# Moving one weight-conversion step behind two output copies in a hand-written engine schedule

## The chip, the cores and the metric

The kernel runs on one core of a Trainium2 chip. The metric is the device time of one execution in microseconds (us). Three executions of the kernel before took 1083.78, 1084.74 and 1087.2 us; the median is 1084.74 us.

## The reference

Eight batches of 576 tokens by 512 channels go through three stages:

```python
# attention without a score matrix, 8 heads of 64
q_s = softmax(q, over the head dimension);  k_s = softmax(k, over the tokens)
x = q_s @ (k_s.T @ v)
# first mixer
h = relu(x @ w_in); u, v = h[..., :512], h[..., 512:]
v_n = (v - mean(v)) / sqrt(var(v) + 1e-6)
y1 = (u * (w_spatial @ v_n + b_spatial)) @ w_out
# second mixer
theta = y1 @ w_theta
u = y1 + w_tok_r @ (y1 * cos(theta)) + w_tok_i @ (y1 * sin(theta))
out = u + relu(u @ w_ch)
```

Several weight matrices (`w_in`, `w_out`, `w_theta`, `w_tok`, `w_ch`) are doubles and are sent as their bits; the kernel turns each block of such a matrix into two float32 halves, `hi` and `lo`.

## The kernel before

Each float32 product is made of three passes over such halves (hi by hi, hi by lo, lo by hi). Two phases follow each other. The first runs over the eight batches; in batch b it does the first mixer of batch b and the attention of batch b + 1, with parts of the attention of batch b + 2, and it sends `y1` to DRAM. The second phase runs the second mixer over all batches from there. This study is about the first phase.

The order of all work is written out by hand: each batch has a string of words, and one word stands for one step, a Python function that issues instructions to several engines. Every engine takes its own instructions in the order in which the words issue them. Batch 0 runs `PLANS[0]`, batch 1 `PLANS[1]`, batches 2 to 6 `PLAN` and batch 7 `LAST`. The steps that matter here:

- `Y0` to `Y3` (`y_mm`, helper line 164): the products with `w_out`, 24 matrix products (of 288 columns) each, into a PSUM tile of two banks. The pool of these tiles has three buffers, shared by all large products (`V`, `K`, `U`, `S`, `T`, `X`, `Y`).
- `y0` to `y3` (`y_out`, L555 and L556): ScalarE copies the PSUM tile of `Yi` to SBUF, into one of nine buffers of a pool called `t2`, and SyncE's queue sends it to DRAM. The copy is what frees the PSUM tile.
- `X3` and `x3` (L164; L437, L438, L456): a product of the attention, and its split by a ScalarE copy and VectorE operations. `X1`, `x1`, `X2` and `x2p` are alike; with the flag `p`, ScalarE also copies the tile out of PSUM (L435) and GpSimd does the subtraction.
- `B` (`Convert.bits`, lines 214 to 245): the first step of a weight block's conversion. In the form used here VectorE does L219, L225, L229 and L241, and ScalarE L223 (behind L219) and L232 (behind L229); L241 comes behind L223. It takes three `t2` buffers. Then `bits` lets SyncE's queue load the block that will be wanted two steps later (L212).
- `P0v` and `P` (`Convert.parts`): the second step of a conversion: ScalarE L257, VectorE L258 and the product L261, which VectorE does with the flag `v` and GpSimd without; for blocks kept for the second phase two DMAs to DRAM follow (L263, L264).
- `ksub2` (L321, L326) and `qsub2` (L399): large subtractions on GpSimd; `kmb2` (L313) a ScalarE copy ahead of `ksub2`; `qmax2` (L394) a VectorE reduction ahead of `qsub2`; `kexp2` (L333) and, in the next batch, `qexp1` (L402) exponentials on ScalarE behind them.
- `V0`, `V1`, `V2`, `K1` open the next batch on TensorE (L172 and L350); `v0` to `v2` (L477) are the ScalarE copies that free their tiles.

In `PLAN` the batch ends with "... `G3v P0v kbc2 kmb2 ksub2 Y0 B Y1 y0 X3 x3 y1 qmax2 qsub2 Y2 kexp2 Y3 y2 P0v y3`". There are 35 weight blocks in all, and each `B` takes the next one; by the count of the words they are used up within batch 6, before the `B` between `Y0` and `Y1`, which then does nothing. Batch 6 also has no `kmax2` to `kexp2`, since there is no batch 8.

Of the kernel before, what the change touches and what calls it, by code (L numbers as in the profile page):

```python
# [17 lines left out]
P = 128  # L18
MAGIC = 12582912.0
# [4 lines left out]
HALF_PI = 1.5707963267948966  # L24
# 896 float32 exponents: a double's bias less a float32's.
REBASE = -896.0 * 2**23


# The first phase's schedule.
KCUTS = (0, 2048, 1024, 1536)  # L30
# [11 lines left out]
)  # L42
# [23 lines left out]
def kernel(  # L66
# [12 lines left out]
):  # L79
    """float32 products run as three float32r passes: x = hi + lo with hi = x rounded to  # L80
    float32r and lo = x - hi (exact), and x @ y = hi@hi + hi@lo + lo@hi."""
    nc = tc.nc
    B = q.shape[0]
    S = w_tok.shape[2]
# [14 lines left out]
    def psum(two, one):  # L99
        """PSUM for a phase: `two` buffers of two banks, `one` of a single bank."""  # L100
        pools.close()
        for n, bufs in (("two", two), ("one", one)):
            ps_now[n] = pools.enter_context(
                tc.tile_pool(name=f"ps_{n}{two}", bufs=bufs, space=bass.MemoryType.PSUM)
            )
# [9 lines left out]

    # Buffers of the first phase; the second one takes them over when they fall free.
    w4_all = fix.tile([P, 8, 1024], F32R, name="w4")
# [41 lines left out]
    def acc(ps, pairs, first=True, final=True):  # L159
        """ps += lhsT.T @ rhs over the pairs, the free size in two halves."""  # L160
        last = len(pairs) - 1
        for i, (a, w) in enumerate(pairs):
            for c in range(2):
                nc.tensor.matmul(  # L164
                    out=ps[:, c, 0:CH], lhsT=a, rhs=w[:, c * CH:(c + 1) * CH],
                    start=first and i == 0, stop=final and i == last,
                )
# [11 lines left out]

# [1 line left out]
    class Split:  # L181
        """A float32 matrix from DRAM, split: hi and lo are where the halves go."""

# [15 lines left out]
    class Convert:  # L199
        """A double matrix from DRAM, given as its bits, split. The exponent, rebased as a number  # L200
        (below float32's range it comes to zero), and the first 11 mantissa bits are hi; the other
        bits, times hi's power of two, are lo."""

# [61 lines left out]

# [1 line left out]
    def load(to, x, n, cuts=(0,)):  # L267
        """The columns from each cut to the next."""
        if n < B:
            ends = sorted(cuts)[1:] + [x.shape[2]]  # L270
            for c in cuts:
                e = ends[sorted(cuts).index(c)]
                nc.sync.dma_start(out=to[:, c:e], in_=x[n][:, c:e])
# [42 lines left out]
    def k_sub(n, hs, eng):  # L316
        """Half h: heads 4h to 4h + 3."""
        mb = st["mb"]
        c = slice(hs[0] * 256, (hs[-1] + 1) * 256)
        km = kb[:, 0:2048].rearrange("p (r c) -> p r c", r=NT)[:, :, c]  # L320
        eng.tensor_tensor(  # L321
            out=km, in0=km, in1=mb[:, :, c].to_broadcast([P, NT, c.stop - c.start]), op=ALU.subtract
        )
        for h in hs:
            p0, c0 = h * 64, h * 256
            eng.tensor_tensor(  # L326
                out=kb[p0:p0 + 64, 2048:2304], in0=kb[p0:p0 + 64, 2048:2304],
                in1=mb[p0:p0 + 64, 0, c0:c0 + 256], op=ALU.subtract,
            )
# [100 lines left out]
    def split(ps, h, l, eng):  # L430
        """ps as hi and lo; GpSimd, which has no way to PSUM, needs a copy."""
        if eng is nc.gpsimd:
            x = t2()
            x = halves(x) if len(ps.shape) == 3 else x
            nc.scalar.copy(out=x, in_=ps)  # L435
            ps = x
        nc.scalar.copy(out=h, in_=ps)  # L437
        eng.tensor_tensor(out=l, in0=ps, in1=f(h), op=ALU.subtract)  # L438

    def q_t_split(n, j, eng):  # L440
        ps = st.pop(("T", j))
        # The first batch has a buffer more, where w_out comes later.
        h, l = qt_s[j % 2 * 2:j % 2 * 2 + 2] if n or j < 2 else [w[:, 0:S] for w in wo[j * 2 - 4:j * 2 - 2]]
        split(ps[:, 0:S], h, l, eng)
        st["qt", j] = h, l
# [11 lines left out]

# [1 line left out]
    def v_mm(t):  # L459
# [97 lines left out]

# [1 line left out]
    y1 = [t.rearrange("p (k s) -> p k s", k=NK) for t in (qb, kb)]  # L559
    z_rem = [vn[8:10]]  # L560

    def zs(b, t):
        """(hi, lo) of zr and of zi. The first batch's come while the first phase still needs
        w_out, some of them where w_ch comes after them."""
        if t < 2:
            z = vn[4 * t:4 * t + 4]
        else:
            z = [w[:, 0:DM] for w in w4[4 * t - 8:4 * t - 4]]
            if b:
                z = [w[:, h * DM:(h + 1) * DM] for w in wo[2 * t - 4:2 * t - 2] for h in range(2)]  # L570
        return z[0:2], z[2:4]
# [15 lines left out]

    # The last tokens of two batches share a tile.
    def load_rem(b):
# [28 lines left out]
    def th_whole(b, t):  # L618
        """Whole turns in theta, plus MAGIC."""
        ps = th[b, t]  # L620
        r, w = t2(DM), t2(DM)
        nc.scalar.activation(out=w, in_=ps, func=ACTF.Copy, scale=INV_2PI, bias=MAGIC)
        th[b, t] = ps, r, w

    def th_turns(b, t):
        """theta less whole turns, in [-pi, pi]."""
        ps, r, w = th[b, t]
        nc.vector.tensor_scalar(out=w, in0=w, scalar1=-MAGIC, scalar2=None, op0=ALU.add)
        nc.vector.scalar_tensor_tensor(out=r, in0=w, scalar=-TWO_PI_HI, in1=ps, op0=ALU.mult, op1=ALU.add)
        nc.vector.scalar_tensor_tensor(out=r, in0=w, scalar=-TWO_PI_LO, in1=r, op0=ALU.mult, op1=ALU.add)  # L630
        nc.vector.tensor_scalar(
            out=r, in0=r, scalar1=PI_BELOW, scalar2=-PI_BELOW, op0=ALU.min, op1=ALU.max
        )
        th[b, t] = r, w
# [49 lines left out]
    def theta(b, i):  # L684
        """Step i of a batch's theta: the products of tile i, and what follows them for the tiles
        before it."""
        if b < B:
            for lag, part in (
                (3, th_y), (0, th_mm), (1, th_whole), (2, th_trig), (4, th_hi),
                (3, th_z), (1, th_turns), (4, th_lo),  # L690
            ):
                if 0 <= i - lag < NT + (b % 2 == 0):
                    part(b, i - lag)

    def tok_mm(b, m, part=None):
        """In parts: the products whose weights come first, the others."""
        c = slice(m * P, (m + 1) * P)
# [23 lines left out]
    def ch_mm(b, m):  # L721
# [5 lines left out]
        if (b, m) != (B - 1, NK - 1):  # L727
# [6 lines left out]
            return  # L734
        # The very last: half of it is on its way while the other half is computed.
        for c in (slice(0, CH), slice(CH, S)):
# [8 lines left out]
    w_out_k = w_out.rearrange("k p f -> p k f")  # L745
    # The first phase's weights; ORDER has them in the order in which it needs them.
    w1 = {}
# [10 lines left out]
    first = [w1[n] for n in ORDER.split()]  # L758
    # The second phase's, kept in DRAM until their buffers fall free.
    later = [  # L760
# [18 lines left out]

    # A batch's schedule is made of words NAME[DIGIT[FLAGS]]. DIGIT is a tile, or for the  # L780
    # attention's own steps the batch's distance. Flags: v and p have a step done by the vector
    # engine or by GpSimd, a and b one half of it.
    def eng(fl, other=nc.gpsimd):
# [102 lines left out]
def _rows(a):  # L886
    """[B, H, S, D] -> [B, 128, R]: whole tiles of 128 tokens as (tile, head, d), then the
    last 64 tokens, heads 0-3 on partitions 0-63 and heads 4-7 on partitions 64-127."""
    import numpy as np
# [8 lines left out]
def _rows_v(a):  # L898
    """The same tokens with a one after each head's row; the last tile holds each head's rows
    on the partitions where q and k have them and zeros on the others."""  # L900
    import numpy as np
# [59 lines left out]
```

## Time and profile before

| | |
|---|---|
| timed executions | 1083.78, 1084.74, 1087.2 us |
| profiled execution, span from the first to the last instruction | 1082.7 us |
| median of the timed executions less that span | 2.0 us |
| TensorE busy / weight loads | 94% / 88% of the span |
| VectorE / ScalarE / GpSimd busy | 62% / 39% / 35% |
| mean granted TensorE clock | 0.972 |

The profiled execution is known by its span; its own time with what lies around the span is not given, and the timed executions are 1.1 to 4.5 us above the span. The granted clock is a share of full speed, 2.4 GHz; the other level is 1.2 GHz. Busy shares are averages over stages with different limits, so the stage at a batch's end is read by itself.

### The profile page before, as it was taken

To read this page: it belongs to the slowest core of one execution; us is meant where nothing else is said; L and a number is where in the kernel's file an instruction comes from. 1 tells how busy PE (TensorE), PEld (TensorE's weight loads), DVE (VectorE), ACT (ScalarE), POOL (GpSimd) and SP (SyncE) were. 2 spreads that over 40 slices of the span, in tenths; PEclk is the share of its full clock that TensorE was granted. 3 is DMA by queue.
4 is the path that set the end of the run, shared out by engine and by line. 5 is a ranking of instruction groups with operands and counts; after the bars stand their busy time and mean duration, and the time that the engine had idled before them with its cause. 6 is when DMAs were issued, how large, how long until landed. Compare 5 with 4: busy or idle time off the path is not lost.

```text
span 1082.7 us, 16227 instructions
## 1 busy us (share of the span) xinstructions
PE 1018.7 (94%) x6688; PEld 952.1 (88%) x6688; DVE 674.9 (62%) x971; ACT 420.1 (39%) x674; POOL 383.7 (35%) x287
## 2 busy tenths in 40 slices
PE   4777799999898998998999999999999999999998
PEld 3666789989798898898999989999999899989998
DVE  7988847866767668677642582738473746366532
ACT  3644345444443353344432461415141424152310
POOL 5466515542444334434521241413131213222220
PEclk9878899999999899998999999999999999999999
DMA  8442122422342233413015041702020101011011
GB/s 278 142 136 99 61 88 121 169 115 86 110 159 77 91 146 107 157 58 131 3 49 185 24 166 76 175 1 74 15 77 22 56 34 65 33 49 41 1 45 44
DMA packets 37369, 96.49 MB, mean 89 GB/s; under 512 B 7088, under 2 KB 15792, under 8 KB 33200
## 3 DMA queue, kind: packets, MB, share of 16 engines
q1 hardware_dynamic: 33744, 85.96, 22.0%
q0 software_dynamic: 3552, 9.50, 3.1%
q8 instruction: 52, 0.85, 0.3%
q14 instruction: 21, 0.17, 0.0%
HBM read 67.08 MB, written 28.38 MB: 88 GB/s over the span
## 4 chain that ended last, share of the span: by engine, by line
PE 72%; DVE 5%; issue 3%; ACT 1%; ACTq 0%
PE ps L164 50%; PE pb L172 10%; PE ps L172 7%; PE ps L350 3%; PE pb L646 1%; DVE t L282 1%; PE ps L425 1%; DVE t L258 1%; DVE t L287 1%; DVE t L219 0%; DVE t L225 0%; PE ps L427 0%; DVE t L539 0%; ACT t L555 0%; DVE t L229 0%
## 5 line engine op out<-in xcount | busy, mean ns | idle before, releaser
L164 PE MATMUL ps<-sp,vn 128*128 128x288 f32 x1472 | 212.6, 301 | 7.0 <-ACT vn L505 3.0
L164 PEld LDWEIGHTS ps<-sp,vn 128*128 128x128 f32 x1472 | 203.5, 193 | 9.1 <-ACT vn L505 3.4
L164 PE MATMUL ps<-g,wo 128*128 128x288 f32 x1104 | 169.7, 308 | 19.8 <-ACT t L555 19.7
L164 PEld LDWEIGHTS ps<-g,wo 128*128 128x128 f32 x1104 | 159.9, 200 | 21.7 <-ACT t L555 21.1
L719 POOL TENSOR_TENSOR qt<-u,uh 128x576 fp32r<-128x576 f32 x31 | 44.2, 1427 | 218.0 <-ACT uh L717 218.0
L717 ACT CAST uh<-u 128x576 fp32r<-128x576 f32 x32 | 21.6, 674 | 216.3 <-DVE u L714 216.3
L172 PE MATMUL ps<-w,xh 128*128 128x512 f32 x320 | 100.6, 408 | 2.9 <-ACT w L257 2.9
L164 PE MATMUL ps<-xh,w 128*128 128x288 f32 x512 | 92.7, 300 | 4.1 <-ACT w L257 2.3
L164 PE MATMUL ps<-uh,w 128*128 128x288 f32 x496 | 91.8, 299 | 0.0
L164 PEld LDWEIGHTS ps<-xh,w 128*128 128x128 f32 x512 | 77.5, 191 | 6.1 <-ACT w L257 2.9
L172 PE MATMUL pb<-w,xh 128*128 128x512 f32 x256 | 81.3, 398 | 0.0
L172 PEld LDWEIGHTS ps<-w,xh 128*128 128x128 f32 x320 | 61.0, 194 | 17.8 <-ACT w L257 3.2
L541 POOL TENSOR_TENSOR g<-t,g 128x576 fp32r<-128x576 f32 x24 | 35.9, 1494 | 112.0 <-ACT g L540 93.0
L164 PEld LDWEIGHTS ps<-uh,w 128*128 128x128 f32 x496 | 73.6, 188 | 0.3
L488 POOL TENSOR_TENSOR mv<-mv,neg_half 128x1 f32<-128x1 f32 (+1 forms) x40 | 27.1, 688 | 125.4 <-DVE mv L487 117.2
L714 DVE TENSOR_TENSOR u<-ps,kb 128x576 f32<-128x576 f32 x16 | 12.1, 758 | 74.0 <-PE ps L164 74.0
L484 DVE BATCH_NORM_STATS2 sm<-t 128x6 f32<-128x512 f32 (+1 forms) x40 | 27.3, 684 | 47.3 <-ACT t L477 41.7
L172 PEld LDWEIGHTS pb<-w,xh 128*128 128x128 f32 x256 | 47.0, 188 | 9.9
L164 PE MATMUL ps<-xl,w 128*128 128x288 f32 x256 | 55.5, 299 | 0.0
L540 ACT CAST g<-t 128x576 fp32r<-128x576 f32 x32 | 21.5, 673 | 84.8 <-DVE t L539 84.8
L164 PE MATMUL ps<-sp,wo 128*128 128x288 f32 x336 | 53.8, 296 | 0.0
L164 PE MATMUL ps<-qt,w 128*128 128x288 f32 x248 | 53.0, 295 | 0.0
(203 smaller groups left out, 2081.9 us busy)
## 6 DMA issues: line engine op xcount, KB each, us to landing
vb<-in_v SPq DMA_DIRECT2D x8, 1300.0 KB, 7.0
y<-t SPq DMA_DIRECT2D x32, 288.0 KB, 2.1
out<-t SPq DMA_DIRECT2D x31, 288.0 KB, 2.1
qb<-in_q SPq DMA_DIRECT2D x7, 1152.0 KB, 5.0
kb<-in_k SPq DMA_DIRECT2D x6, 1152.0 KB, 7.9
st<-in_w_tok SPq DMA_DIRECT2D x9, 576.0 KB, 4.1
tok_d<-st SPq DMA_DIRECT2D x18, 288.0 KB, 2.1
qb<-y SPq DMA_DIRECT2D x4, 1152.0 KB, 5.2
```

What stands on the lines that cost most here:

```text
L164: nc.tensor.matmul(out=ps[:, c, 0:CH], lhsT=a, rhs=w[:, c * CH:(c + 1) * CH], start=first and i == 0, stop=final and i == last,)
L172: nc.tensor.matmul(out=ps, lhsT=a, rhs=w, start=(i == 0), stop=(i == last))
L258: nc.vector.tensor_scalar(out=w.bitcast(I32), in0=a.bitcast(I32), scalar1=-0x800000, scalar2=None, op0=ALU.bitwise_and)
L282: nc.vector.tensor_tensor(out=m[p0:p0 + 64, c0:c0 + 256], in0=m[p0:p0 + 64, c0:c0 + 256], in1=kb[p0:p0 + 64, 2048:2304], op=ALU.max,)
L350: nc.tensor.matmul(out=o, lhsT=kb[p, c0:c0 + P], rhs=v4[p, r, 2 * j:2 * j + 2, :].rearrange("p h e -> p (h e)"), start=(r == 0), stop=(r = ...
L484: nc.vector.bn_stats(out=bs[0:n], in_=vr[0:n])
L488: nc.gpsimd.tensor_tensor(out=mv[0:n, 1:2], in0=mv[0:n, 1:2], in1=neg_half[0:n, 0:1], op=ALU.pow)
L540: nc.scalar.copy(out=g_s[m], in_=g)
L541: eng.tensor_tensor(out=g_s[4 + m], in0=g, in1=f(g_s[m]), op=ALU.subtract)
L714: nc.vector.tensor_tensor(out=halves(u_s[m]), in0=ps[:, :, 0:CH], in1=halves(y1[b % 2][:, m, :]), op=ALU.add)
L717: nc.scalar.copy(out=st["uh"][:, m, :], in_=u_s[m])
L719: eng.tensor_tensor(out=qt_s[m], in0=u_s[m], in1=f(st["uh"][:, m, :]), op=ALU.subtract)
```

## The change

In `PLAN` and in `PLANS[0]` the word `B` is taken from its place ahead of `y0` (`PLAN`) or between `y0` and `y1` (`PLANS[0]`) and put behind `y1`. `PLANS[1]` and `LAST` stay. No step is added or removed. The diff also blanks comments and docstrings, line for line, so that line numbers stay.

```diff
 PLAN = (
...
-    "t3p kr2 S3 G3v P0v kbc2 kmb2 ksub2 Y0 B Y1 y0 X3 x3 y1 qmax2 qsub2 Y2 kexp2 Y3 y2 P0v y3 "
+    "t3p kr2 S3 G3v P0v kbc2 kmb2 ksub2 Y0 Y1 y0 X3 x3 y1 B qmax2 qsub2 Y2 kexp2 Y3 y2 P0v y3 "
 )
 PLANS = {
     0: (
...
-        "x0 T1 kt2 kr2 Y0 t1p kbc2 kmb2 T2 t2 ldv2 y0 B ksub2 Y1 X1 y1 P X2 x1 x2p Y2 y2 T3 ldq2 Y3 "
+        "x0 T1 kt2 kr2 Y0 t1p kbc2 kmb2 T2 t2 ldv2 y0 ksub2 Y1 X1 y1 B P X2 x1 x2p Y2 y2 T3 ldq2 Y3 "
         "t3p X3 y3 x3 qmax2 qsub2v "
     ),
```

## Rows read from the trace of the kernel before

**Rows 1.** The page: span, busy times, and one line of its DMA issues (KB each, us to landing).

```profile
span 1082.7 us, 16227 instructions
...
PE 1018.7 (94%) x6688; PEld 952.1 (88%) x6688; DVE 674.9 (62%) x971; ACT 420.1 (39%) x674; POOL 383.7 (35%) x287
...
st<-in_w_tok SPq DMA_DIRECT2D x9, 576.0 KB, 4.1
```

**Rows 2.** Waits of PE, 60 to 600 us: total us, times, longest.

```profile
PE ps L164 <- ACT t L555: 19.5, 5, 4.1
```

**Rows 3.** Chain that ended last, end of batch 2: start, us, what.

```profile
276.00 0.97 DVE t L219
...
279.29 0.63 ACT t L555
...
288.13 8.41 PE ps L172 x36
```

**Rows 4.** Timeline of PE, ends of batches 2 to 6: start, us, instructions [idle before].

```profile
268.40 6.63 PE L164 MATMUL ps<-g,wo 128*128 128x288 f32 x48
...
279.96 8.16 PE L164 MATMUL ps<-g,wo 128*128 128x288 f32 x48 [4.14 <-ACT t L555]
...
353.29 9.13 PE L164 MATMUL ps<-g,wo 128*128 128x288 f32 x48 [4.14 <-ACT t L555]
...
427.56 7.97 PE L164 MATMUL ps<-g,wo 128*128 128x288 f32 x48 [4.14 <-ACT t L555]
...
500.38 9.00 PE L164 MATMUL ps<-g,wo 128*128 128x288 f32 x48 [3.83 <-ACT t L555]
...
561.71 6.56 PE L164 MATMUL ps<-g,wo 128*128 128x288 f32 x48
```

**Rows 5.** Timeline of ACT, end of batch 2.

```profile
277.01 0.78 ACT L223 ACTIVATE t<-t,rebase 128x576 int32<-128x576 int32 x1 [6.24 <-DVE t L219]
...
280.87 2.15 ACT L333 ACTIVATE kb<-kb 128x2304 f32<-128x2304 f32 x1
...
288.70 2.13 ACT L402 ACTIVATE qb<-qb 128x2304 f32<-128x2304 f32 x1
290.97 0.60 ACT L477 ACTIVATE t<-ps 128x512 f32<-128x512 f32 x1
```

**Rows 6.** Timeline of DVE, end of batch 2.

```profile
270.90 5.17 DVE L261 TENSOR_TENSOR st<-t,t 128x576 fp32r<-128x576 f32 x1
...
278.58 0.75 DVE L241 SCALAR_TENSOR_TENSOR t<-st,t 128x576 int32<-128x576 int32 x1
...
281.39 2.54 DVE L394 TENSOR_REDUCE q_m<-qb 128x36 f32<-128x2304 f32 x1
```

**Rows 7.** Timeline of POOL, end of batch 2.

```profile
270.85 4.62 POOL L321 TENSOR_TENSOR kb<-kb,t 128x2048 f32<-128x2048 f32 x1 [3.12 <-ACT t L313]
275.42 2.14 POOL L326 TENSOR_TENSOR kb<-kb,t 64x256 f32<-64x256 f32 x2
284.17 4.06 POOL L399 TENSOR_TENSOR qb<-qb,q_m 128x2304 f32<-128x2304 f32 x1 [6.61 <-DVE q_m L394]
```

**Rows 8.** Stretches: us, busy PE, PEld, DVE, ACT, POOL, granted clock, DMA share, GB/s.

```profile
194.84:204.00 9.16, 9.16 (x70) 9.16 (x71) 6.39 (x10) 4.04 (x8) 5.74 (x4) 1.00 0.66 237
279.96:288.12 8.16, 8.15 (x49) 8.16 (x50) 7.56 (x5) 4.27 (x5) 3.96 (x1) 0.79 0.38 145
```

**Rows 9.** Timeline of PE, end of batch 0 and, last row, end of batch 1.

```profile
127.69 3.45 PE L164 MATMUL ps<-g,wo 128*128 128x288 f32 x24
...
136.02 4.97 PE L164 MATMUL ps<-g,wo 128*128 128x288 f32 x24 [3.29 <-ACT t L555]
...
194.84 0.66 PE L294 MATMUL pb<-ident,t 128*128 128x128 f32 x4 [1.26 <-DVE t L287]
```

**Rows 10.** Timeline of ACT, end of batch 0.

```profile
135.34 0.62 ACT L555 COPY t<-ps 128x576 f32<-128x576 f32 x1
...
136.91 0.65 ACT L435 COPY t<-ps 128x576 f32<-128x576 f32 x1
```

## The prediction

> **What bounds the kernel now.** The page comes first: TensorE is busy for 1018.7 of 1082.7 us, while VectorE, ScalarE and GpSimd stay at 62% and below [rows 1]. So time is gained only where TensorE stands still or runs slowly. The table of TensorE's waits in the first phase comes next, and one line leads it: five times, 19.5 us in all, the products of line 164 waited for a ScalarE instruction of L555, the y copy [rows 2]. The timeline of TensorE says where. In each of batches 2 to 5 the 48 products of `Y2` and `Y3` begin behind an idle stretch of 4.14, 4.14, 4.14 and 3.83 us, and the fifth wait, 3.29 us, stands ahead of `Y2` in batch 0 [rows 4, 9]. Each time the PSUM tile that `Y2` needs is not yet copied out.
>
> Why is the copy late? In batch 2 `Y0` and `Y1` run from 268.40 to 275.03 [rows 4], so `Y0`, the first half, is through at about 271.7. The chain that ended last starts the copy of `y0` only at 279.29 [rows 3]. In between, ScalarE stands idle for 6.24 us until L219 on VectorE is done, and runs L223 at 277.01 [rows 5]; L219 starts at 276.00 [rows 3], because the product L261 ahead of it takes from 270.90 to 276.07 [rows 6] while GpSimd's subtraction L321 runs from 270.85 to 275.47 [rows 7]. ScalarE works in order: `y0`'s copy, whose data lie ready, is queued behind the two ScalarE instructions of `B`, and those wait for VectorE.
>
> The idle time has a second price. After it the same 48 products take 8.16, 9.13, 7.97 and 9.00 us, against 6.56 us in batch 6, where `B` has no block left and no wait comes first [rows 4]. The stretch of 8.16 us shows a granted clock of 0.79 of full speed [rows 8]: part of it ran at the lower of the two levels, 1.2 GHz. In batch 0 `Y2` alone takes 4.97 us against 3.45 us of `Y1` [rows 9].
>
> **The change in batches 2 to 5.** Nothing is added or removed. `B`'s two ScalarE instructions now stand behind the copies of `y0`, `x3` and `y1`, its four VectorE instructions behind `x3`'s, and its load behind two DMAs on SyncE's queue; GpSimd gets nothing in this form of `B`.
> - ScalarE: `y0`'s copy needs only `Y0` and a free buffer. It runs at about 271.8 to 272.4, as soon as `Y0` is through, in what is now idle time.
> - TensorE: `X3` ends at 275.82 (279.96 less 4.14) and `Y2` can follow at once. `Y3` needs `y1`'s copy: behind `x3`'s ScalarE copy that ends at about 277.1, and `Y3` wants it at 275.82 + 6.56 / 2 = 279.1. No new wait.
> - Gain of idle time: 4.14 + 4.14 + 4.14 + 3.83 = 16.25 us. Gain of speed, once no idle time comes first: 8.16 + 9.13 + 7.97 + 9.00 less 4 times 6.56 = 8.02 us. Together 24.3 us.
>
> Is the gain kept? TensorE enters `V0` 5.7 us earlier in batch 2, at 275.82 + 6.56 = 282.4 instead of 288.13 [rows 3], but the other engines do not all move by that much. `V0` to `V2` take 8.41 us [rows 3]; `K1` then wants, at 290.8, the tile that `v0`'s copy frees. That copy stands on ScalarE behind the exponential of q, that behind GpSimd's subtraction, that behind `qmax2`, that behind `B`. `B`'s four VectorE instructions take 3.3 us now, from 276.00 [rows 3] to the end of L241 at 279.33 [rows 6]; the first two run beside the end of L326 [rows 7], and are longer than L241's 0.75 us. In the new place they begin behind `x3`'s operations, at about 277.5 (an estimate: `X3`'s end at 275.82, a ScalarE copy and two VectorE operations of 0.2 to 0.75 us), when L326 ends at 277.56. At 0.75 us each they take 3.0 us, at the most the old 3.3; I take 3.0, since GpSimd is then idle. Then `qmax2` 2.54 us [rows 6] to 283.0, GpSimd 4.06 us [rows 7] from 283.2 to 287.3 (the 0.2 us as now), the exponential 2.13 us and the copy 0.60 us [rows 5]: `v0` is copied at 290.0, 0.8 us before `K1` wants it, or 0.5 us with the old 3.3. So I book nothing here, with a bound of 1.5 us a batch, should GpSimd be later. The k exponential, 2.15 us [rows 5], is behind `B` in both orders and ends before the copy of `y2` is wanted by `V1`, at 285.2.
>
> The load of a later weight block is issued about 1 us later, behind the DMAs of `y0` and `y1`. Such a load lands after 4.1 us [rows 1], and its block is wanted by the second `B` from there, in the middle of a next batch that lasts 73 us (279.96 to 353.29 in rows 4). Cost nothing; without that cover it would be the 1 us.
>
> **Batch 0.** `y1`'s copy moves ahead of `B`. It ran at 135.34 [rows 10]; `Y1` ends at 131.14 [rows 9], so it can be done at 131.8. `Y2` then starts when `X2` is through, at 132.73 (136.02 less 3.29), takes 3.45 us and ends at 136.2. But `T3` behind it needs the tile that `x2p`'s copy L435 frees. That copy, at 136.91 now [rows 10], stays behind `B`'s ScalarE work and moves only by the `y1` copy that no longer stands ahead of it, about 0.5 us: it ends at 137.1. TensorE is at `T3` at 137.1, where it now is at 136.02 + 4.97 = 141.0, or about 0.2 us earlier by the overlap of successive instructions: gain 3.7 us, where `Y2`'s wait and speed alone would give 3.29 + 4.97 - 3.45 = 4.8. Batches 1, 6 and 7 keep their order, and batch 6's moved `B` is empty.
>
> **The sum.** 24.3 + 3.7 = 28.0 us off the profiled span of 1082.7 us. The median of the timed runs lies 2.0 us above that span; I take that as constant: 1084.74 - 28.0 = 1056.7 us.
>
> **Two rules weighed.** First, the clock. A TensorE idle stretch of 1.26 us at the end of batch 1 [rows 9] is followed by 9.16 us at clock 1.00 [rows 8]; the five long ones of [rows 4, 9] are followed by slow products. I take it that the 1 us of idle time that I leave in batch 0 costs no speed. The Trainium skill, in "TensorE: Matmul & The Clock Gate", section "A second HAM failure mode: psum-queue depth-cycling", says that short idle gaps between groups of products that cycle through PSUM make the clock go back and forth; by that, products would stay slow here even where the long wait is gone. The 1.26 us row speaks against it. Second, the neighbours of `B`. L261 takes 5.17 us [rows 6] beside GpSimd's subtraction, and L241, of the same size, 0.75 us after it. The Trainium skill's "GPSIMD Engine Reference", section "8. Key points", says that GpSimd shares its SBUF interfaces with VectorE and contends with instructions that read two SBUF inputs or run in a two-port mode; by that rule a `B` that met a GpSimd subtraction in its new place would stretch in the same way, and the last rival below is what that would do.
>
> **The rivals.**
> - *The copies get buffers that are not free.* `y0` and `y1` now take their `t2` buffers ahead of `B`, so others than before. If they are those that L261 reads, `y0`'s copy waits until 276.07 and ends at 276.75, `Y2` starts at 276.8, and each of four batches loses 1.0 us: 24.0 us gained, 1060.7 us. For it: nine buffers, and L261 is late. Against it: buffers of the earlier gate steps should be free for longer.
> - *The idle time goes but the speed stays low.* Then 16.25 us in batches 2 to 5 and 3.3 us in batch 0 are gained, 19.5 us: 1065.2 us. Against it the 1.26 us row; for it nothing but the page.
> - *The change does nothing:* `Y2` is held by something that ends when the copy did. Then 1084.7 us. Against it: ScalarE's 6.24 us of idle time, with `Y0` long through.
> - *Slower: the conversion holds up `qmax2`.* If `B`'s VectorE instructions met GpSimd's subtractions in the new place and were held for all of 4.62 + 2.14 + 4.06 = 10.8 us [rows 7], `v0`'s copy would be 10.8 us later than the 290.0 above and TensorE would wait 10.8 - 0.8 = 10.0 us at `K1` in each of four batches: 40.0 less 24.3 less 3.7 = 12.0 us slower, 1096.7 us. It decides from a delay of 0.8 + 28.0 / 4 = 7.8 us on. Against it: L326 ends at 277.56, where `B` begins, and the q subtraction cannot start before `qmax2`, behind `B`.
>
> **How the numbers follow.** Forecast 1056.7 us, chance 0.72, own range 1053.5 to 1059. Buffers 0.13, speed stays low 0.08, no effect 0.04, slower 0.03. The range goes down to 1053.5, for the 0.9 us by which timed runs lie below their median and 2 us by which modelled product ends hide idle time, and up to 1063, over the buffer rival and over a `K1` wait of up to 1.5 us in four batches; it leaves out about 0.15 to 0.2. About 0.3% (3.3 us) is what a measurement of this kernel can tell from no change: faster 0.94, same 0.03, slower 0.03.
>
> **What would show it.** Right: the line of waits for L555 falls from 19.5 us to about 1 us or vanishes; the 48 products of `Y2` and `Y3` take 6.6 us at clock 1.00 in batches 2 to 5; `y0`'s copy starts within 0.3 us of the end of `Y0`; in batch 0 a wait of about 1 us for L435 stands ahead of `T3`; ends of batches are shorter by 5 to 7 us. Wrong: a wait of `K1` or `V3` for L477, a `y0` copy that starts behind L261, or a `Y2` at a clock below 1.00. The prediction fails if a later stage of the batch (the gate, `T0`, `S0`) turns out to wait for GpSimd or VectorE, which move less than TensorE does.

## The result

The changed kernel takes 1060.15 us, the median of four executions (1059.61 to 1061.09), beside 1084.32 us of the kernel before (also four): a ratio of 0.9772, with a 95% interval of 0.9758 to 0.9787. The forecast was 1056.7 us. The measured time lies outside the range that the forecast gave its own theory, 1053.5 to 1059, and inside the wide one, up to 1063, which also covers a rival and a wait at `K1`. The profiled span falls from 1082.7 to 1057.8 us, 24.9 us less where 28.0 were forecast.

The page of the changed kernel, span and busy times, beside [rows 1]:

```profile
span 1057.8 us, 16239 instructions
...
PE 1009.8 (95%) x6688; PEld 943.1 (89%) x6688; DVE 676.4 (64%) x971; ACT 419.3 (40%) x674; POOL 383.6 (36%) x287
```

TensorE's waits from 60 to 600 us (total us, times, longest us), beside [rows 2]:

```profile
...
PE ps L425 <- POOL vn L506: 1.6, 3, 0.5
PE ps L425 <- ACT t L435: 1.3, 1, 1.3
PE ps L164 <- DVE qt L438: 1.0, 4, 0.3
PE ps L164 <- ACT u L524: 0.9, 4, 0.2
...
```

The line of 19.5 us for L555 is gone. In its place stand two lines that the kernel before did not have in the steady batches, L425 behind L506 and L164 behind L524, and the 1.3 us behind L435 that the forecast left in batch 0. The line for L438, 1.0 us, is in both kernels. The longer lines, left out here, are waits of batch 0 ahead of `Y0` in both kernels; `K1` of batch 0 starts at 96.59 us before and at 96.76 us after.

The timeline of TensorE in the changed kernel, ends of batches 2 and 3, then batch 0, beside [rows 4, 9]:

```profile
264.69 6.63 PE L164 MATMUL ps<-g,wo 128*128 128x288 f32 x48
271.15 0.69 PE L164 MATMUL ps<-qt,kvh 128*128 128x288 f32 x4
...
271.95 6.56 PE L164 MATMUL ps<-g,wo 128*128 128x288 f32 x48
...
340.48 6.56 PE L164 MATMUL ps<-g,wo 128*128 128x288 f32 x48
...
132.47 3.35 PE L164 MATMUL ps<-g,wo 128*128 128x288 f32 x24
...
137.10 0.66 PE L425 MATMUL ps<-ident,qb 128*128 128x128 f32 x4 [1.28 <-ACT t L435]
```

`Y2` follows `X3` at once, and its 48 products with `Y3` take 6.56 us, the time of an undisturbed batch. The table of stretches of the changed kernel, from the first products of `Y0` to the end of `Y3` in batches 2 and 3 (us, busy PE, PEld, DVE, ACT, POOL, granted clock, DMA share, GB/s), beside [rows 8], say at which clock:

```profile
264.93:278.50 13.57, 13.57 (x103) 13.57 (x103) 12.27 (x12) 7.39 (x10) 6.56 (x3) 1.00 0.37 130
333.46:347.04 13.58, 13.58 (x104) 13.58 (x103) 12.28 (x12) 7.40 (x10) 6.56 (x3) 1.00 0.37 132
```

The timeline of ScalarE in the changed kernel, end of batch 2, beside [rows 5]:

```profile
268.21 0.64 ACT L555 COPY t<-ps 128x576 f32<-128x576 f32 x1 [1.15 <-PE ps L164]
272.15 0.64 ACT L437 CAST xh<-ps 128x576 fp32r<-128x576 f32 x1 [3.30 <-PE ps L164]
272.68 0.64 ACT L555 COPY t<-ps 128x576 f32<-128x576 f32 x1
274.23 0.78 ACT L223 ACTIVATE t<-t,rebase 128x576 int32<-128x576 int32 x1 [0.90 <-DVE t L219]
```

and that of VectorE there, beside [rows 6]:

```profile
267.19 5.17 DVE L261 TENSOR_TENSOR st<-t,t 128x576 fp32r<-128x576 f32 x1
```

VectorE's L261 takes the same 5.17 us, from 267.19 to 272.36, but `y0`'s copy no longer waits for it: it starts at 268.21, as soon as TensorE has ended `Y0`. So the rival with buffers that are not free is out as well: had the copy needed a buffer that L261 reads, it could not have started before 272.36.

Where does the rest go? The table takes the point where the V products begin on the chain that ended last as the bound of a batch. In batch 2 the chain joins them in both kernels only at the last product of `V0`, which waits 0.48 us; `V0` itself begins there at 213.87 and 210.21, which gives the same gain.

| | before | after | gained | forecast |
|---|---|---|---|---|
| chain at `V0`, batch 2 (gain of batches 0 and 1) | 217.09 | 213.42 | 3.67 | 3.7 |
| batch 2 | 71.04 | 65.08 | 5.96 | 4.14 + 1.60 = 5.74 |
| batch 3 | 74.29 | 68.54 | 5.75 | 4.14 + 2.57 = 6.71 |
| batch 4 | 73.11 | 68.53 | 4.58 | 4.14 + 1.41 = 5.55 |
| batch 5 | 73.85 | 68.42 | 5.43 | 3.83 + 2.44 = 6.27 |
| batch 6 | 66.09 | 66.58 | -0.49 | 0 |

Batches 0 to 2 give what was forecast. Batches 3 to 6 give 0.96, 0.97, 0.84 and 0.49 us less, 3.3 us together. These are the batches that begin behind a shortened end; batch 2 begins behind batch 1, which keeps its order. The middle of batch 5 shows the place, in the timeline of TensorE of the changed kernel:

```profile
447.97 0.63 PE L425 MATMUL ps<-ident,qb 128*128 128x128 f32 x4 [0.52 <-POOL vn L506]
448.53 0.27 PE L427 MATMUL ps<-ident,qb 64*128 64x64 f32 x1
449.03 3.99 PE L164 MATMUL ps<-sp,vn 128*128 128x288 f32 x28 [0.23 <-ACT u L524]
```

`T0` waits 0.52 us and `S0` 0.23 us, where the kernel before waits at neither. Read backwards, the trace gives this chain. The PSUM tile of `T0` is the one that `r1` (L524) frees, that of `S0` the one that `r2` frees. These copies stand on ScalarE behind the copies of `N3` and `N4` (L505, L508, L509), those wait for L500 on VectorE, and VectorE is late since an operation of `kn1`, L382. The timelines of VectorE and GpSimd in the changed kernel, batch 5 (the L500 shown is the last that `r1` and `r2` stand behind):

```profile
430.43 0.88 DVE L375 TENSOR_TENSOR kn<-ps,sm 64x256 f32<-64x256 f32 x2
431.33 2.71 DVE L382 TENSOR_TENSOR kvl<-kn,kvh 64x256 fp32r<-64x256 f32 x2
...
443.98 2.10 DVE L500 TENSOR_SCALAR t<-t,mv 128x512 f32<-128x512 f32 x2
...
429.25 4.06 POOL L420 TENSOR_TENSOR qb<-qb,q_s 128x2304 f32<-128x2304 f32 x1
```

and the same instructions, without L375, in the kernel before:

```profile
451.29 1.10 DVE L382 TENSOR_TENSOR kvl<-kn,kvh 64x256 fp32r<-64x256 f32 x2
...
462.38 2.10 DVE L500 TENSOR_SCALAR t<-t,mv 128x512 f32<-128x512 f32 x2
...
447.61 4.05 POOL L420 TENSOR_TENSOR qb<-qb,q_s 128x2304 f32<-128x2304 f32 x1
```

The pair of L382 ends 0.73 us behind the end of GpSimd's q multiplication L420 in both kernels (434.04 and 433.31; 452.39 and 451.66). TensorE has moved forward by more than GpSimd: TensorE goes on from `K1` 2.1 us behind the start of L420 before (449.70 and 447.61) and 0.5 us behind it after (429.74 and 429.25). So the subtraction, which comes right behind `K1`, now meets the multiplication and waits for its end: 2.71 less 1.10, 1.6 us later, of which about 1.0 us a batch reaches TensorE. On the way the lateness is passed on whole: from the end of the pair to the end of L500 it takes 12.04 us after (446.08 less 434.04) and 12.09 us before (464.48 less 452.39).

### The profile page after: what moved, and what is told of

Same layout as the page of the kernel before. It is cut to its first block, busy times and chain, and to the rows that moved or that the text cites. A ratio compares the mean times of both kernels' runs of the same rounds, so it can differ in the third digit from the quotient of the medians.

```text
span 1057.8 us, 16239 instructions
## 1 busy us (share of the span) xinstructions
PE 1009.8 (95%) x6688; PEld 943.1 (89%) x6688; DVE 676.4 (64%) x971; ACT 419.3 (40%) x674; POOL 383.6 (36%) x287
## 3 DMA queue, kind: packets, MB, share of 16 engines
q1 hardware_dynamic: 33744, 85.96, 22.6%
## 4 chain that ended last, share of the span: by engine, by line
PE 69%; DVE 8%; ACT 3%; issue 2%; ACTq 0%
PE ps L164 48%; PE pb L172 10%; PE ps L172 6%; PE ps L350 3%; PE pb L646 1%; DVE t L500 1%; DVE kvl L382 1%; DVE t L282 1%; ACT u L524 1%; ACT vn L505 1%; DVE sm L484 1%; DVE t L287 1%; DVE t L258 0%; PE ps L425 0%; DVE qt L438 0%
## 5 line engine op out<-in xcount | busy, mean ns | idle before, releaser
L164 PE MATMUL ps<-sp,vn 128*128 128x288 f32 x1472 | 213.1, 301 | 9.7 <-ACT t L477 3.8
L164 PEld LDWEIGHTS ps<-sp,vn 128*128 128x128 f32 x1472 | 203.8, 193 | 12.2 <-ACT t L477 4.3
L164 PE MATMUL ps<-g,wo 128*128 128x288 f32 x1104 | 160.1, 296 | 0.2 <-ACT t L555 0.2
L164 PEld LDWEIGHTS ps<-g,wo 128*128 128x128 f32 x1104 | 150.9, 189 | 0.7 <-ACT t L555 0.4
L717 ACT CAST uh<-u 128x576 fp32r<-128x576 f32 x32 | 21.6, 673 | 216.3 <-DVE u L714 216.3
L164 PE MATMUL ps<-xh,w 128*128 128x288 f32 x512 | 91.6, 297 | 4.8 <-POOL w L261 2.4
L164 PE MATMUL ps<-uh,w 128*128 128x288 f32 x496 | 91.8, 299 | 0.0
L164 PEld LDWEIGHTS ps<-xh,w 128*128 128x128 f32 x512 | 76.3, 188 | 6.8 <-POOL w L261 3.1
L164 PEld LDWEIGHTS ps<-uh,w 128*128 128x128 f32 x496 | 73.6, 188 | 0.3
L164 PE MATMUL ps<-xl,w 128*128 128x288 f32 x256 | 54.9, 296 | 0.0
L164 PE MATMUL ps<-sp,wo 128*128 128x288 f32 x336 | 53.8, 296 | 0.0
L164 PE MATMUL ps<-qt,w 128*128 128x288 f32 x248 | 53.0, 295 | 0.0
L714 DVE TENSOR_TENSOR u<-ps,qb 128x576 f32<-128x576 f32 x16 | 12.1, 758 | 63.5 <-PE ps L164 63.5
```

What stands on the lines that cost most here:

```text
L164: nc.tensor.matmul(out=ps[:, c, 0:CH], lhsT=a, rhs=w[:, c * CH:(c + 1) * CH], start=first and i == 0, stop=final and i == last,)
L714: nc.vector.tensor_tensor(out=halves(u_s[m]), in0=ps[:, :, 0:CH], in1=halves(y1[b % 2][:, m, :]), op=ALU.add)
L717: nc.scalar.copy(out=st["uh"][:, m, :], in_=u_s[m])
```

## The experiments

The theory has two parts. First, the order of ScalarE's queue made the stall: a y copy waits for whatever stands ahead of it there, and the slow products follow from the stall. Second, the missing 3.3 us are VectorE's subtraction held by GpSimd's multiplication. The rivals are given with each run. The kernel before, run beside the experiments, had medians of 1084.13, 1085.63 and 1084.3 us in the three groups.

**One plan at a time.** In the first kernel only `PLAN` is changed, in the second only `PLANS[0]`.

```diff
 e1, against the changed kernel
-... y0 ksub2 Y1 X1 y1 B P X2 ...
+... y0 B ksub2 Y1 X1 y1 P X2 ...
 e2, against the changed kernel
-... ksub2 Y0 Y1 y0 X3 x3 y1 B qmax2 ...
+... ksub2 Y0 B Y1 y0 X3 x3 y1 qmax2 ...
```

> The move in the steady plan alone; batch 0's plan as before. Theory (each plan's gain is its own stall and adds): batch 0 loses its 3.7 us again, so 1060.2 + 3.7 = 1063.8 us, with the 2.2 us stall of batch 0 back and no wait on a y copy in batches 2 to 5. Rival (the two moves help each other, or batch 0's gain is eaten later): 1060.2, or more than 1065.

> The move in batch 0's plan alone; the steady plan as before. Theory: 1084.3 - 3.7 = 1080.6 us, and the stalls of 4.1 us stand in batches 2 to 5 as before. Rival (batch 0's gain is given back where batch 1 waits for something else): 1084.3.

Measured: 1064.14 us (ratio 0.9817, 0.9801 to 0.9834) and 1081.48 us (0.9975, 0.9963 to 0.9987). The gains of 20.0 and 2.65 us (interval 1.4 to 4.0) add up to 22.6 us beside 24.2 of the whole change; the interval of the first, 18.0 to 21.6 us, and that of the second leave room for the rest. TensorE's waits with only `PLAN` changed:

```profile
PE ps L164 <- ACT t L555: 3.3, 1, 3.3
```

and with only `PLANS[0]` changed:

```profile
PE ps L164 <- ACT t L555: 16.3, 4, 4.1
```

Each part takes away its own stalls and leaves the other's. The stall of batch 0 is 3.3 us, as in the kernel before, and not the 2.2 us of the expectation.

**Only the first copy ahead.** The step stands behind `y0`, but ahead of `x3` and `y1`.

```diff
-... Y0 Y1 y0 X3 x3 y1 B qmax2 ...
+... Y0 Y1 y0 B X3 x3 y1 qmax2 ...
```

> In the steady plan the step stands behind the first y copy only, ahead of the next batch's x split and the second y copy. Theory (ScalarE works in order, and what it has queued ahead of a y copy decides when the next output tile may start): the first wait is gone, and the second y copy now comes some 3 us later, at 1 us or less behind the moment at which TensorE wants its buffer: a new wait of 0.5 to 2 us ahead of the fourth output tile in each of batches 2 to 5, 1062 to 1068 us. Rival (the place of the first copy alone counts): 1060.2 and no wait on a y copy.

Measured: 1065.27 us (0.9832, 0.9814 to 0.9851), 5.1 us more than the changed kernel by the medians. The waits of TensorE in this kernel:

```profile
PE ps L164 <- ACT t L555: 6.0, 4, 1.6
```

Its timeline of TensorE at the end of batch 2:

```profile
272.65 3.36 PE L164 MATMUL ps<-g,wo 128*128 128x288 f32 x24
277.58 3.46 PE L164 MATMUL ps<-g,wo 128*128 128x288 f32 x24 [1.58 <-ACT t L555]
```

Its timeline of ScalarE there:

```profile
275.78 0.68 ACT L232 ACTIVATE t<-t 128x576 f32<-128x576 uint32 x1 [1.00 <-DVE t L229]
276.37 0.62 ACT L437 CAST xh<-ps 128x576 fp32r<-128x576 f32 x1
276.89 0.64 ACT L555 COPY t<-ps 128x576 f32<-128x576 f32 x1
```

The stretch behind the wait, in the columns of the stretches above (the granted clock is 1.00):

```profile
277.50:281.00 3.50, 3.42 (x25) 3.42 (x26) 3.43 (x5) 3.16 (x4) 0.29 (x1) 1.00 0.24 91
```

The stall has moved from `Y2` to `Y3`: `y1`'s copy now stands behind L232 and starts at 276.89, where the changed kernel has it at 272.68. So it is the place in ScalarE's queue that counts, for each copy by itself, and the rival is refuted. The waits are 6.0 us, and in return the 1.6 us at `T0` are gone in the next batches; together that would be 4.4 us, and what makes up the rest was not followed. The last row adds that after 1.58 us of standing still the clock is 1.00, and the 24 products take 3.46 us, as `Y1` of batch 0 does without a wait before it [rows 9].

**Still later.** The step stands behind GpSimd's q subtraction.

```diff
-... x3 y1 B qmax2 qsub2 Y2 kexp2 ...
+... x3 y1 qmax2 qsub2 B Y2 kexp2 ...
```

> In the steady plan the step stands still later, behind the q maximum and GpSimd's q subtraction. Theory (VectorE's operations on SBUF are held up beneath a long GpSimd operation, and ScalarE's k exponential, third y copy and q exponential are queued behind the step): the third y copy comes some 5 us later and the q exponential about 2.5 us later, new waits of 2 to 6 us at the turn of each steady batch, 1068 to 1085 us. Rival (any place behind the second y copy is as good): 1060.2, or about 2 us a batch less, since the q maximum and subtraction start earlier.

Measured: 1079.52 us (0.9962, 0.9948 to 0.9977), 19.4 us more than the changed kernel, 4.8 us for each of four batches. The timeline of GpSimd in this kernel, end of batch 2:

```profile
276.37 4.05 POOL L399 TENSOR_TENSOR qb<-qb,q_m 128x2304 f32<-128x2304 f32 x1 [2.74 <-DVE q_m L394]
```

VectorE beside it:

```profile
276.43 4.31 DVE L225 TENSOR_SCALAR t<-st 128x576 int32<-128x576 int32 x1
280.77 0.76 DVE L229 SCALAR_TENSOR_TENSOR t<-st,t 128x576 int32<-128x576 int32 x1
```

ScalarE behind these:

```profile
282.22 2.11 ACT L333 ACTIVATE kb<-kb 128x2304 f32<-128x2304 f32 x1
284.23 0.62 ACT L555 COPY t<-ps 128x576 f32<-128x576 f32 x1
```

TensorE, in the next batch's `V1`:

```profile
284.90 0.73 PE L172 MATMUL ps<-w,xh 128*128 128x512 f32 x2 [3.73 <-ACT t L555]
```

Two stretches behind that wait:

```profile
285.00:288.00 3.00, 3.00 (x9) 2.38 (x10) 0.00 (x0) 3.00 (x4) 0.00 (x0) 0.66 0.78 296
288.00:292.00 4.00, 4.00 (x16) 3.18 (x15) 2.72 (x7) 1.07 (x2) 1.10 (x2) 0.83 0.21 77
```

This is the forecast's slower rival in a milder form, brought about by the order of the words. `B`'s L225 takes 4.31 us beneath the subtraction (0.45 us in the changed kernel), the k exponential and `y2`'s copy are queued behind the step, the copy starts at 284.23 instead of 278.06, and TensorE stands still for 3.73 us in the next batch's `V1`. Here the clock falls to 0.66 and 0.83 behind the wait.

**The multiplication earlier.** In `PLAN`, `qmul1` goes ahead of the third V tile's statistics, whose small GpSimd operation stood in front of it.

```diff
-... qsum1 V2 v2 qmul1 K1 ldv2 kn1 ...
+... qsum1 V2 qmul1 v2 K1 ldv2 kn1 ...
```

> The changed kernel, and in the steady plan GpSimd's q multiplication ahead of the third V tile's statistics step instead of behind it: it starts some 1 to 1.5 us earlier. Theory (the 3.3 us that the forecast lacks come from the k normalisation's subtraction on VectorE, which waits for the end of that multiplication, 2.71 us a pair where it was 1.10): the pair goes back to about 1.1 to 1.6 us, TensorE's waits of 0.5, 0.2 and 0.3 us a batch go, and the time falls by 2 to 3.3 us to 1057 to 1058. Rival (the waits come with the earlier start of the batch and have another cause): 1060.2.

> The kernel of e5 itself, beside e8 on one chip: 1056.5 to 1057 by every theory; with e5's own four runs it says what the earlier q multiplication is worth.

Measured: 1056.47 us (0.9743, 0.9726 to 0.976) and, beside the last experiment, 1057.09 us (0.9748, 0.9734 to 0.9761). The changed kernel itself was run beside the first:

> The changed kernel itself, beside e5 to e7 on one chip: 1060.2 by every theory.

It took 1060.24 us (0.9773, 0.9759 to 0.9787). Beside it the earlier multiplication is worth 3.8 us by the medians; by the ratios to the kernel before it is 3.3 us in this group and 2.7 us with the repeat. That is about the 3.3 us that were missing. VectorE and GpSimd in batch 5 of this kernel:

```profile
429.54 1.30 DVE L382 TENSOR_TENSOR kvl<-kn,kvh 64x256 fp32r<-64x256 f32 x2
...
426.05 4.05 POOL L420 TENSOR_TENSOR qb<-qb,q_s 128x2304 f32<-128x2304 f32 x1 [2.61 <-DVE q_s L415]
```

The pair is back at 1.30 us and once more ends 0.74 us behind L420 (430.84 and 430.10); the waits of `T0` are gone, and that for L524 falls from four to one, of 0.2 us. From `K1` of batch 2 to `K1` of batch 6 this kernel takes 489.45 - 219.26 = 270.19 us, the changed kernel 492.23 - 219.36 = 272.87: 2.68 us less, where the table lacks 0.96 + 0.97 + 0.84 = 2.77 us in these batches. In batch 5 all of it lies where the chain says: from the start of `K1` to the start of `S0` it is 446.23 - 422.02 = 24.21 us here and 449.03 - 423.82 = 25.21 us in the changed kernel.

**The control.** The same edit in the kernel before.

> Control: the kernel before with the same earlier q multiplication as in e5. Theory (there the multiplication ended just as the k subtraction began, so nothing is held up): 1084.3, the same. Rival (the earlier multiplication is a gain of its own, whatever the change does): 1081 to 1082.

Measured: 1085.48 us, ratio 1.0001 (0.999 to 1.0011): the same. The earlier multiplication pays only where TensorE arrives early, so the 3.3 us are a cost that the change itself uncovered.

**Who is waited for at `T0`.** The profile names GpSimd's L506 ahead of `T0`; by the chain above it is ScalarE's `r1`. In this kernel `r1` goes ahead of `N3` and `N4`.

```diff
-... U2 N3 N4 r1 U3 P0v r2 ...
+... U2 r1 N3 N4 U3 P0v r2 ...
```

> The changed kernel, and in the steady plan the copy of the second U tile ahead of the last two V normalisations on ScalarE. Theory (the first q transposition waits for the PSUM buffer of that copy, which is queued on ScalarE behind work that waits for VectorE; the profile's GpSimd is only the name of the last semaphore): the wait of 0.5 us at the transposition goes in batches 3 to 5, the wait for the third copy stays at about 0.2: 1.5 to 2 us less than the changed kernel, 1058.2 to 1058.7. Rival (the transposition waits for GpSimd's low part of V, as the profile says): 1060.2 and the 0.5 us stay.

Measured: 1059.55 us (0.9766, 0.9752 to 0.978), 0.7 us less than the changed kernel beside it by the medians, which is not clear of noise. The timeline of TensorE in batch 5:

```profile
447.31 0.60 PE L425 MATMUL ps<-ident,qb 128*128 128x128 f32 x4
447.84 0.27 PE L427 MATMUL ps<-ident,qb 64*128 64x64 f32 x1
448.52 3.98 PE L164 MATMUL ps<-sp,vn 128*128 128x288 f32 x28 [0.41 <-ACT u L524]
...
453.54 0.80 PE L164 MATMUL ps<-qt,kvh 128*128 128x288 f32 x4 [0.40 <-DVE qt L438]
```

The timeline of GpSimd there:

```profile
446.38 1.29 POOL L506 TENSOR_TENSOR vn<-t,vn 128x512 fp32r<-128x512 f32 x1 [1.02 <-ACT vn L505]
```

The wait at `T0` is gone, and `T0` starts at 447.31, before L506 ends at 447.67: the name in the wait's row was the wrong one. But the 1.5 to 2 us that were expected are not there: from `K1` of batch 2 to `K1` of batch 6 it takes 492.19 - 219.29 = 272.90 us, beside 272.87 in the changed kernel. `S0` now waits 0.41 us for `r2`, and `X0` 0.40 us for VectorE's L438, which stands behind the same late VectorE work. The waits for L438 rise from 1.0 us in four to 2.6 us in eight. One late engine holds TensorE at several points; to free one of them hands the time to the next.

**The 1.3 us in batch 0.** The kernel of the earlier multiplication, with `B` and the `P` behind it moved past the x splits, so that the copy L435 comes sooner.

```diff
-... Y1 X1 y1 B P X2 x1 x2p Y2 y2 ...
+... Y1 X1 y1 X2 x1 x2p B P Y2 y2 ...
```

> The kernel of e5, and in batch 0 the conversion step, with the parts step that follows it, behind the two x splits instead of ahead of them. Theory (the 1.3 us that TensorE still waits at the last q transposition of batch 0 is ScalarE's copy for the second x split, queued behind the step): that wait goes, 1.3 us less than e5: 1055 to 1055.5. Rival (the parts step, now later, or the third y copy, now behind the step, holds something up): 1056.5 or more, with a new wait in batch 0 or 1.

Measured: 1059.55 us (0.9764, 0.9749 to 0.9778), 2.5 us more than its base beside it (1057.09) by the medians, with intervals that overlap; the traces show the loss plainly, 153.92 - 128.56 = 25.36 us from the start of `Y1` to `K1` of batch 1, beside 151.72 - 128.94 = 22.78 in the base. TensorE in batch 0:

```profile
136.64 0.60 PE L425 MATMUL ps<-ident,qb 128*128 128x128 f32 x4
137.17 0.27 PE L427 MATMUL ps<-ident,qb 64*128 64x64 f32 x1
139.51 0.82 PE L164 MATMUL ps<-g,wo 128*128 128x288 f32 x4 [2.07 <-ACT wo L257]
140.74 4.16 PE L164 MATMUL ps<-g,wo 128*128 128x288 f32 x20 [0.41 <-POOL wo L261]
```

`T3` no longer waits, as expected; but `Y3` behind it now waits 2.07 and 0.41 us for `wo`, the very block that these two steps convert. The rival with the later `P` came true, and the instruction that waits, which the rival left open, is `Y3`: in batch 0 the step is not only in the way of others, it has a due time of its own.

## Why the prediction was right, and where it was off

- **How far the number speaks for it.** The forecast missed by 3.4 us, and its own theory's range, up to 1059 us, did not hold. The wide range did, by a bound for a wait at `K1` that did not come and by a rival (1060.7 us, buffers that are not free) that the copy's start at 268.21 refutes. That the measured time lies within 0.6 us of that rival, and in the range, is in part luck; the signs in the trace, below, are what bears the theory out.
- **What bounds the kernel** and the cause of the stall held: with `y0` and `y1` ahead of the step the waits for L555 are gone, the part-by-part runs show each stall with its own part, and the run with the step between the copies shows the rule again on `y1`.
- **The gain of idle time and of speed, 24.3 us**, is there at the ends of the batches in full: 6.56 us at clock 1.00 in each. That the speed follows from the long wait, as forecast against the speed rival and the page "TensorE: Matmul & The Clock Gate" of the Trainium skill (section "A second HAM failure mode: psum-queue depth-cycling"), is what the experiments show too. By that section short idle gaps between groups of products would make the clock go back and forth; here, at the batches' ends, a gap of 1.58 us leaves it at 1.00, and one of 3.73 us is followed by 0.66. In batch 0 shorter gaps were followed by slow products as well (last section), so the runs do not rule that section out there.
- **Batch 0, 3.7 us:** 3.67 measured, with the 1.28 us wait behind L435 that was left in the sum. From `Y1` of batch 0 to `K1` of batch 1 it is 26.34 us before and 22.78 after, 3.56 us; the last 0.1 us arose ahead of the edit. The step held.
- **`K1`:** no wait. `v0` and `v1` are both copied by 285.90, 0.85 us before `K1` starts at 286.75; the forecast had 0.8 us for the first of them. It gave `B` 3.0 us on VectorE; it takes 2.28 us, from 273.74 to 276.02.
- **The step that failed is "So I book nothing here".** The forecast looked for the late engines at `K1`'s PSUM tile, found 0.8 us to spare, and took the gain as kept from there on. It followed the q chain only as far as the copy of `v0` on ScalarE. The same chain goes on to GpSimd's q multiplication, which starts 1.6 us later with respect to `K1` than before and holds VectorE's first SBUF subtraction behind `K1`. That term measures 0.96 + 0.97 + 0.84 + 0.49 = 3.3 us in batches 3 to 6. Its place, `T0` and `S0`, was named in the last sentence as one by which the prediction fails, but given no price; by that sign, and by batch 4, which gains 4.58 us where 5 to 7 were the sign, this part did fail, though the time fell in the range. With 24.3 + 3.7 - 3.3 = 24.7 us the sum meets the 24.9 us of the spans.
- **The neighbours.** The Trainium skill's "GPSIMD Engine Reference", section "8. Key points", says that GpSimd contends with VectorE instructions that read two SBUF inputs or run in a two-port mode. L382 reads two tiles in SBUF and is held; L375, which reads one of its inputs from PSUM, takes 0.88 us beside the same multiplication, and 0.87 us in the control's batch 5, where the multiplication has ended. This agrees. The forecast used the rule on `B` alone, and the rule bit on another instruction half a batch later.

## What to carry to other kernels

When a change moves the engine that bounds the kernel forward by several us, list what the others do in the next stages with respect to it, not only at the first meeting point: a chain that moves less slides beneath instructions that it used to miss, and the price appears where in-order queues pass it on. A step taken out of a copy's way goes into a window with two edges, here `y1`'s copy on one side and GpSimd's subtraction, or the step's own due time, on the other; both edges have a price that the profile shows. And a wait row can name an engine that was not the one waited for; then look at what stands ahead in another queue; to move that one instruction tells who it was, though not what the whole lateness is worth.

## What the runs showed of the hardware that was not expected

- A VectorE operation with a single SBUF input was held as well: `B`'s L225, one input and one output in SBUF, took 4.31 us beneath GpSimd's 4.05 us subtraction, and 0.45 us in the changed kernel. The forecast had the whole of `B` stretch, and did not say which of its operations would.
- Standing still does not cost clock in proportion: behind 1.58 us the granted clock was 1.00, behind 3.73 us 0.66 and then 0.83, part of the time at the lower level. The length of one wait does not settle it. In the second profile of the earlier multiplication's kernel TensorE did nothing from 119.4 to 123.0 us in batch 0 but nine transpositions (L425, L427, L294), with waits of 1.90 and 0.35 us; `Y0` behind them took 4.97 us, with a granted clock of 0.66 from 125 to 128 us:

```profile
121.97 0.66 PE L294 MATMUL pb<-ident,t 128*128 128x128 f32 x4 [1.90 <-DVE t L287]
122.97 4.97 PE L164 MATMUL ps<-g,wo 128*128 128x288 f32 x24 [0.35 <-DVE t L539]
```

- Two executions of one kernel differ in where in batch 0 the clock drops: in the first profile of the same kernel `S3` took 5.50 and `Y0` 3.45 us, in the second 3.98 and 4.97 us. The products are slow for about as long in both, but ahead of `Y0` TensorE waits for VectorE's L287 anyway (0.37 us in the first, 1.90 us in the second), which takes up the delay of `S3` and not that of `Y0`. `K1` of batch 1 started at 150.28 and 151.72 us, which is all of the difference between these two executions (1056.39 and 1057.79 us). No edit here reaches that far ahead in batch 0. Whether other executions differ by the same is not shown.
